# A gated mix of two attention blocks: the last output tile in pieces of 512, 256, 128 and 128 columns

## Chip, cores and metric

The kernel runs on one core of a Trainium2 chip. The metric is the device time of one execution in microseconds (us); less is better. The median of four runs before the change is 482.8 us (482.68 to 483.35).

## What is computed

The input is 2048 rows of 1024 numbers in bf16. Two blocks read it: A, a linear attention with 32 heads of 32, and B, an attention over a window of eight keys, every second one back. Each ends in a product with its own matrix `wo`, and a gate per row mixes them.

```python
def reference(A_x, A_wqkv, A_wo, B_x, B_wqkv, B_wo, gate_w):
    ...
    x = A_x
    g = _sigmoid((x * gate_w).sum(-1, keepdims=True))
    a = _A_ref(x, A_wqkv, A_wo)
    b = _B_ref(x, B_wqkv, B_wo)
    return g * a + (1 - g) * b
```

Both `_A_ref` and `_B_ref` end in `o.reshape(B, S, D) @ wo`. The change touches the last step alone: block B's product with its `wo`, and the sum of both blocks.

## The kernel before, in words

**Stages.** The rows are held transposed, features on the 128 partitions. The kernel computes B's values, queries and keys, then A's keys and values in stretches shared with B's window attention, then A's numerators. `a_out` (line 1722) makes A's gated output and leaves it in `pq0` and `xT`. `final(t)` (line 1736) makes 128 rows of the result and stores them. There are NT = 16 such tiles; the first five are built before the last calls of `a_out`, and tiles 5 to 15 (line 1801) close the program.

**One tile.** `final` cuts the tile's 1024 columns into parts. For each part TensorE (PE) runs eight matmuls that sum over the eight chunks of 128 features into one PSUM bank (line 1747; `qT` holds B's attention output, `ws[3]` holds B's `wo`). Each matmul has a weight load of 128 x 128 of its own, so a part is 16 instructions for PE, however many columns it has. VectorE (DVE) then computes bank times (1 - gate) plus A's part into an SBUF tile `o` (lines 1751 to 1754). A DMA (line 1757) writes `o` to the output. Tiles 0 to 14 have two parts of 512 columns and one DMA of 1024 columns, issued by SyncE (SP). The last tile has three parts, 512, 256 and 256, and a DMA for each: SP issues the first two, ScalarE (ACT) the third, because line 1757 gives ACT the part that ends at column 1024. Each first column has a semaphore of its own (`chan="out%d_%d"`).

**Order.** `Prog.schedule` (line 122) lays all operations out on a model clock, by the costs written beside them, and each engine gets its list in that order. `plan` runs six times, and the layout with the shortest modelled span is kept (lines 1811 to 1816). PSUM banks come from `Pool.next`; from line 1644 on there are eight of them.

**The tail.** A flag says whether a fast way of computing is allowed for this input; if it isn't, a general path of many instructions runs. Each engine's program therefore ends in a branch (lines 1820 to 1834):

```python
    def tail(e, eng, rest):
        reg = e.alloc_register("fast_ok")
        e.wait_ge(*flag_op.val)
        e.reg_load(reg, flag[0:1, 0:1])
        with e.If_eq(reg, 0):
            rest()
            ...
            for th in progs[eng]:
                th(e)
        with e.Else():
            rest()
            if eng == "sp":
                for s, v in P.last:
                    e.wait_ge(s, v)
```

`rest()` is what of the engine's list starts in the last microseconds of the modelled span, so many as `BACK` (line 22) has: 19 for SP, 14 for DVE, 30 for ACT. Operations before that are issued ahead of the branch (line 254). PE has no entry there, so all of PE's work is issued before its branch, and its `rest()` is empty. The taken side, `Else`, lies behind the general path in the program. At the end SP waits for the output DMAs (line 1834), and all engines meet at the end of the block (line 1836).

Of the kernel before, what the change touches and what calls it, by code (L numbers as in the profile page):

```python
# [1116 lines left out]
def build_kernel(nc, A_x, A_wqkv, A_wo, B_x, B_wqkv, B_wo, gate_w, out):  # L1117
    del B_x
    S = A_x.shape[1]
    NT = S // 128  # L1120
# [118 lines left out]
    def plan(seen):  # L1239
# [476 lines left out]
        def a_loc(t):  # L1716
            tgt, c0 = pqn(t // 4)
            return tgt, c0 + (t % 4) * 128
# [17 lines left out]
        def final(t):  # L1736
            tgt, c0 = a_loc(t)
            o_, os_ = osb.next()
            e_, r = t // 8, t % 8
            parts = [(0, 512), (512, 1024)] if t < NT - 1 else [(0, 512), (512, 768), (768, 1024)]  # L1740
            for f0, f1 in parts:
                bank = main.next()
                n = f1 - f0

                def fn(e, t=t, bank=bank, f0=f0, f1=f1):
                    for dc in range(8):
                        last = e.matmul(bank.ap(0, f1 - f0), qT[:, dc, t * 128:(t + 1) * 128], ws[3][:, dc, f0:f1], start=(dc == 0), stop=(dc == 7))  # L1747
                    return last
                P.op("pe", fn, 8 * mm(n), reads=[qT.part((0, 8), (t * 128, (t + 1) * 128)), ws[3].part((0, 8), (f0, f1))], writes=[bank.iv])
                i0, i1 = f0 // 128, f1 // 128  # L1750
                P.op("dve", lambda e, bank=bank, o_=o_, t=t, n=n, i0=i0, i1=i1, tgt=tgt, c0=c0: e.scalar_tensor_tensor(  # L1751
                    out=o_[:, i0 * 128:i1 * 128].rearrange("p (i s) -> p i s", s=128), in0=bank.ap(0, n).rearrange("p (i s) -> p i s", s=128),
                    scalar=gm[:, t:t + 1], in1=tgt[:, i0:i1, c0:c0 + 128], op0=ALU.mult, op1=ALU.add), dps(n),
                    reads=[bank.iv, gm.all(), tgt.part((i0, i1), (c0, c0 + 128))], writes=[o_.part((f0, f1))])
                if t == NT - 1 or f1 == 1024:
                    c = f0 if t == NT - 1 else 0
                    P.op("act" if f1 == 1024 and c else "sp", lambda e, e_=e_, r=r, o_=o_, c=c, f1=f1: e.dma_start(out2[e_, r * 128:(r + 1) * 128, c:f1], o_[:, c:f1]), 0.5,
                         reads=[o_.part((c, f1))], chan="out%d_%d" % (os_, c), lat=1.0)
# [17 lines left out]
        for t in range(EARLY):  # L1776
            while len(outs) > 16:
                a_out(*outs.pop(0))
            final(t)
# [21 lines left out]
        for t in range(EARLY, NT):  # L1801
            final(t)
# [69 lines left out]
```

## Time and profile before

| What | Value |
|---|---|
| Median of four runs | 482.8 us (482.68 to 483.35) |
| The profiled execution's own time | 483.67 us |
| Its span, first to last instruction | 481.9 us |
| Mean granted TensorE clock | 0.999 |
| PE busy | 477.6 us, 99% of the span, 4403 matmuls |
| DVE, ACT, POOL busy | 281.1, 146.5, 6.2 us |
| Matmuls of `final` (line 1747) | 264, 55.6 us |
| Additions of `final` (line 1751) | 33, of which 2 with 256 columns |
| Output DMAs (line 1757) | 17 on SP, 1 on ACT |

A row of the profile names the engine, the source line, the operation, the tile written and the tile read (`o<-ps_all` reads PSUM and writes `o`), the shape and the count. "PEld" is the weight load of TensorE, which runs beside the matmuls. A `q` behind an engine's name (`SPq`, `PEldq`) marks what the engine's sequencer does by itself: issuing DMAs, waiting for semaphores, loading a register, branching. Such instructions are not counted as busy. Times in the text are microseconds from the start of the span. The trace also holds each packet that a DMA engine moved, with its start, length and bytes; packets of kind "instruction" are pieces of the engines' own programs, fetched while they run.

### The profile page before, as it was taken

The page shows a single profiled execution, that of the slowest core. Times are in us where ns is not written, and L with a number is a line of the kernel's source. Part 1 is how long each engine was busy: PE and PEld are TensorE (multiplying, and loading weights), DVE is VectorE, ACT ScalarE, POOL GpSimd, SP SyncE. Part 2 cuts the span into 40 slices and gives each one's busy share as a digit, 9 for nine tenths or more (in the row PEclk, how much of TensorE's full clock was granted, in tenths as well). Part 3 has the DMA queues.
Part 4 walks back from the last instruction along what each step waited for, and adds up shares of the span by engine and source line. Part 5 has one row for each costly group of instructions (what it writes and reads, how often), then busy time and mean ns, then how long its engine had stood idle before and what let it go on. Part 6 is the DMA issues. An engine that isn't in the chain of part 4 may idle for free.

```text
span 481.9 us, 10218 instructions
## 1 busy us (share of the span) xinstructions
PE 477.6 (99%) x4403; PEld 224.5 (47%) x4403; DVE 281.1 (58%) x578; ACT 146.5 (30%) x234; POOL 6.2 (1%) x38
## 2 busy tenths in 40 slices
PE   8999999999999999999999999999999999999997
PEld 3444444444444544545454455444444444444443
DVE  3121436888587788566747465588588136653444
ACT  1111111135333345434434435255532130111000
POOL 4000000000000000000000000000000000000000
PEclk9999999999999999999999999999999999999999
DMA  9999994132014337432313447820194019830212
GB/s 208 252 210 311 293 353 131 44 112 87 1 31 143 87 91 147 95 81 54 88 38 92 99 123 163 236 45 2 18 246 132 0 19 242 220 23 3 88 68 90
DMA packets 72951, 57.39 MB, mean 119 GB/s; under 512 B 37953, under 2 KB 60865, under 8 KB 72898
## 3 DMA queue, kind: packets, MB, share of 16 engines
q1 hardware_dynamic: 72210, 56.07, 45.2%
q8 instruction: 36, 0.59, 0.5%
q10 hardware_dynamic: 688, 0.59, 0.4%
q14 instruction: 17, 0.14, 0.1%
HBM read 34.49 MB, written 13.76 MB: 100 GB/s over the span
## 4 chain that ended last, share of the span: by engine, by line
PE 99%; DVE 0%; issue 0%
PE ps_all L1344 81%; PE ps_all L1747 11%; PE ps_all L1464 2%; PE ps_all L1499 2%; PE ps_all L1383 1%; PE ps_all L1588 1%; PE ps_all L1692 0%; PE ps_all L1664 0%; DVE o L1751 0%; DVE warm L1290 0%
## 5 line engine op out<-in xcount | busy, mean ns | idle before, releaser
L1344 PE MATMUL ps_all<-w,xT 128*128 128x512 bf16 x960 | 211.5, 380 | 0.0
L1344 PE MATMUL ps_all<-xT,w 128*128 128x512 bf16 x768 | 168.3, 379 | 0.0
L1344 PEld LDWEIGHTS ps_all<-w,xT 128*128 128x128 bf16 x960 | 92.7, 98 | 110.9 <-issue 1.4
L1344 PEld LDWEIGHTS ps_all<-xT,w 128*128 128x128 bf16 x768 | 74.1, 98 | 89.4 <-issue 1.3
L1747 PE MATMUL ps_all<-w,qT 128*128 128x512 bf16 (+1 forms) x264 | 55.6, 373 | 0.0
L1747 PEld LDWEIGHTS ps_all<-w,qT 128*128 128x128 bf16 x264 | 25.8, 98 | 29.7
L1355 DVE TENSOR_SCALAR e<-e 128x512 bf16<-128x512 bf16 x64 | 18.5, 289 | 32.2 <-ACT e L1353 17.4
L1478 ACT ACTIVATE E<-ps_all 128x1824 bf16<-128x1824 f32 (+1 forms) x18 | 30.4, 1687 | 19.0 <-PE ps_all L1499 19.0
L1375 DVE CAST vst<-ps_all 128x512 bf16<-128x512 f32 x16 | 11.1, 694 | 42.4 <-PE ps_all L1344 42.4
L1751 DVE SCALAR_TENSOR_TENSOR o<-ps_all,gm,xT 128x512 bf16<-128x512 f32 (+1 forms) x25 | 18.0, 728 | 21.1 <-PE ps_all L1747 21.0
L1353 ACT ACTIVATE e<-ps_all 128x512 bf16<-128x512 f32 x32 | 19.1, 597 | 31.4 <-PE ps_all L1344 31.4
L1351 ACT ACTIVATE e<-ps_all 128x512 bf16<-128x512 f32 x32 | 19.1, 597 | 26.0 <-PE ps_all L1344 24.8
L1302 DVE TENSOR_TENSOR mx<-mx,kT 128x1024 bf16<-128x1024 bf16 x32 | 20.9, 685 | 9.2 <-ACT kT L1376 9.0
L1516 DVE TENSOR_TENSOR ot<-ps_all,rs 128x480 bf16<-128x480 f32 (+1 forms) x54 | 25.8, 505 | 0.0
L1302 DVE TENSOR_TENSOR mx<-mx,qT 128x1024 bf16<-128x1024 bf16 x32 | 21.0, 684 | 7.3 <-ACT qT L1379 7.1
L1376 ACT ACTIVATE az<-ps_all 128x512 bf16<-128x512 f32 x23 | 13.8, 599 | 36.3 <-PE ps_all L1344 36.3
L1376 ACT ACTIVATE vst<-ps_all 128x512 bf16<-128x512 f32 x16 | 9.6, 599 | 48.1 <-PE ps_all L1344 48.1
L1376 ACT ACTIVATE kT<-ps_all 128x512 bf16<-128x512 f32 x21 | 12.5, 597 | 36.8 <-PE ps_all L1344 36.8
L1379 ACT ACTIVATE qT<-ps_all 128x512 bf16<-128x512 f32 x19 | 11.3, 597 | 35.3 <-PE ps_all L1344 35.3
L1515 DVE RECIPROCAL rs<-ps_all 128x15 f32<-128x15 f32 (+1 forms) x54 | 9.4, 202 | 21.3 <-PE ps_all L1499 19.4
L1357 DVE SCALAR_TENSOR_TENSOR pk<-ps_all,e 128x512 bf16<-128x512 f32 x32 | 21.6, 677 | 0.1
L1379 ACT ACTIVATE xT<-ps_all,g 128x512 bf16<-128x512 f32 x10 | 6.9, 687 | 45.1 <-PE ps_all L1344 42.4
(73 smaller groups left out, 276.5 us busy)
## 6 DMA issues: line engine op xcount, KB each, us to landing
rb<-rc_hbm SPq DMA_DIRECT2D x32, 256.0 KB, 5.9
w<-in_A_wqkv_dram SPq DMA_DIRECT2D x6, 1024.0 KB, 9.4
v<-vB_hbm SPq DMA_DIRECT2D x36, 132.0 KB, 2.7
vB_hbm<-vst SPq DMA_DIRECT2D x32, 132.0 KB, 5.5
w<-in_B_wqkv_dram SPq DMA_DIRECT2D x4, 1024.0 KB, 9.8
xn<-in_A_x_dram SPq DMA_DIRECT2D x16, 256.0 KB, 2.6
out_dram<-o SPq DMA_DIRECT2D x15, 256.0 KB
oB_hbm<-ot SPq DMA_DIRECT2D x36, 96.0 KB, 2.1
```

Source lines behind the costliest of these rows:

```text
L1302: P.op("dve", lambda e, m=m, op=op: e.tensor_tensor(m[:, 0:n], m[:, 0:n], src, op), 0.08 + n / 1920.0, reads=[m.all(), reg], writes=[m.all()],
L1344: last = e.matmul(bank.ap(), lhs(dc), rhs(dc), start=(dc == 0), stop=(dc == 7))
L1351: P.op("act", lambda e: e.activation(e_[:, :], bank.ap(), ACT.Exp), act(512), reads=[bank.iv], writes=[e_.all()])
L1353: P.op("act", lambda e: e.activation(e_[:, :], bank.ap(), ACT.Exp, accum_out=qe[:, col:col + 1]), act(512) + 0.1, reads=[bank.iv], writes= ...
L1355: P.op("dve", lambda e: e.tensor_scalar(e_[:, :], e_[:, :], 1.0, 1e-6, op0=ALU.min, op1=ALU.add), 0.25, reads=[e_.all()], writes=[e_.all()])
L1357: P.op("dve", lambda e: e.scalar_tensor_tensor(out=dst, in0=bank.ap(), scalar=0.0, in1=e_[:, :], op0=ALU.max, op1=ALU.add), dps(512), read ...
L1376: fa = lambda e: e.activation(dst, src(), ACT.Copy)
L1379: fa = lambda e: e.activation(dst, src(), ACT.Copy, scale=scale)
L1478: P.op("act", lambda e: e.activation(E[:, 0:32 * nq].rearrange("p (j q) -> p j q", j=4), ps[:, 4:8, 0:8 * nq], ACT.Exp), act(32 * nq), rea ...
L1516: P.op("dve", lambda e, r=r, src=src, dst=dst, m=m: e.tensor_tensor(dst, src()[:, :, 0:32], r[:, 0:m, None].to_broadcast([128, m, 32]), AL ...
L1747: last = e.matmul(bank.ap(0, f1 - f0), qT[:, dc, t * 128:(t + 1) * 128], ws[3][:, dc, f0:f1], start=(dc == 0), stop=(dc == 7))
L1751: P.op("dve", lambda e, bank=bank, o_=o_, t=t, n=n, i0=i0, i1=i1, tgt=tgt, c0=c0: e.scalar_tensor_tensor(out=o_[:, i0 * 128:i1 * 128].rear ...
```

## The change

The last tile's second block of 512 columns is cut into 256, 128 and 128 columns in place of 256 and 256.

```diff
-            parts = [(0, 512), (512, 1024)] if t < NT - 1 else [(0, 512), (512, 768), (768, 1024)]
+            parts = [(0, 512), (512, 1024)] if t < NT - 1 else [(0, 512), (512, 768), (768, 896), (896, 1024)]
```

What follows from that one line: the part of columns 768 to 1023 becomes two groups of eight matmuls with 128 columns each in place of one group with 256; two additions of 128 columns in place of one of 256; and two DMAs of 128 rows by 256 bytes in place of one of 128 rows by 512 bytes. SP issues the one for columns 768 to 895, ACT the one for 896 to 1023. There is one more bank taken, and one more semaphore for SP to wait for at the end.

## The prediction

> **What bounds the kernel now.** The page comes first: busy time of the engines, then the chain that ended last.
>
> ```profile
> PE 477.6 (99%) x4403; PEld 224.5 (47%) x4403; DVE 281.1 (58%) x578; ACT 146.5 (30%) x234; POOL 6.2 (1%) x38
> ...
> PE 99%; DVE 0%; issue 0%
> ```
>
> TensorE fills the span, and the change leaves its columns as they are. So everything is decided behind the last matmul. The chain in order of time, from 460 us on, and the timeline of the last five microseconds show that stretch:
>
> ```profile
> 459.87 19.03 PE ps_all L1747 x96
> 478.90 0.03 issue
> 478.92 0.48 DVE o L1751
> ```
>
> ```profile
> 478.56 1.27 SPq L1757 DMA_DIRECT2D out_dram<-o  x1
> 478.92 0.48 DVE L1751 SCALAR_TENSOR_TENSOR o<-ps_all,gm,xT 128x256 bf16<-128x256 f32 x1 [0.39 <-PE ps_all L1747]
> 479.44 0.36 ACTq L1757 DMA_DIRECT2D out_dram<-o  x1
> ```
>
> The chain stops at 479.40, yet the span goes on to 481.94. The rest lies in rows that don't count as busy. Asked by source line: the branch (1824), the meeting at the end of the block (1836) and SP's wait for the stores (1834).
>
> ```profile
> L1824 DVEq COMPARE_BRANCH  x1: 72/72/72, 465.7 to 465.7; - x1
> L1824 PEldq COMPARE_BRANCH  x1: 3764/3764/3764, 477.1 to 477.1; - x1
> ```
>
> ```profile
> L1836 PEldq DRAIN  x1: 73/73/73, 480.9 to 480.9; - x1
> L1836 SPq DRAIN  x1: 13/13/13, 481.7 to 481.7; - x1
> ```
>
> ```profile
> L1834 SPq EVENT_SEMAPHORE  x2: 17/22/28, 481.4 to 481.5; - x2
> ```
>
> Two things run side by side to the end. The stores: the last one landed at 481.38, SP passed its waits at 481.40 to 481.49 and reached the meeting at 481.70. And PE's sequencer: its branch began at 477.12 and took 3.76 us, so PE reached the meeting at 480.94 and left its drain at 481.02. The stores came last, PE 0.70 us ahead of them. From the later of the two to the end of the span it was 0.22 us (481.72 to 481.94).
>
> Why 3.76 us? The trace's packets hold one of kind "instruction", 16,384 bytes, on PE's own queue at 478.49 to 479.46: 1.37 us behind the branch's start, and 1.42 us before its end. The branch jumps over the general path to code that isn't there and waits for it. The other engines show the same, hidden behind their 45 to 72 ns: DVE branches at 465.68, its fetch moves at 466.72, its next addition starts at 468.61. That 16 KB packet also hit the stores. One DMA engine carried it, and the eight 1024-byte packets that this engine had of the 512-column store ran from 479.45 to 480.16, where the others were done by 479.25. SP's next store found its queue full and was held:
>
> ```profile
> L1757 SPq DMA_DIRECT2D out_dram<-o x2: 332/800/1267, 478.0 to 478.6; - x2
> L1757 ACTq DMA_DIRECT2D out_dram<-o x1: 365/365/365, 479.4 to 479.4; - x1
> ```
>
> 332 ns is the usual price, 1267 ns that of the held one.
>
> **The change, part by part** (sums against the profiled execution: span 481.94, own time 483.67; that is 0.9 above the median of 482.8, to which I carry over the differences alone).
>
> *Matmuls.* With 512 columns one starts 216 ns after the one before, with 256 columns 109 ns, as these windows show (nine and seventeen starts):
>
> ```profile
> 475.25:476.97 1.72, 1.72 (x9) 0.78 (x8) 0.75 (x1) 0.00 (x0) 0.00 (x0) 1.00 0.00 0
> 476.97:478.72 1.75, 1.75 (x17) 1.46 (x15) 1.24 (x2) 0.00 (x0) 0.00 (x0) 1.00 0.43 159
> ```
>
> That is 0.417 ns per column and about 2.5 ns fixed, so 128 columns should start every 56 ns: 16 x 56 = 0.89 us for 8 x 109 = 0.87 us, +0.02. No row has a full weight load under 128 columns. If loads, 98 ns each, could not overlap at all, it would be 16 x 98 = 1.57 us, +0.70; below, nothing can be had, since the columns stay. I take +0.02, by the 256-column row, whose 109 ns show no trace of its 98 ns load.
>
> The Trainium skill speaks against this: "TensorE: Matmul & The Clock Gate", section "Back-to-back issue gap", gives some 81 ns for a weight load and a matmul of 128 columns. By it the estimate would be 16 x 81 = 1.30 us, +0.42.
>
> *Additions.* 749 ns with 512 columns, 484 with 256: 1.04 ns per column, so 351 ns with 128. The first of the two lies beside the last eight matmuls. The second starts 0.04 behind the last matmul as now and ends 0.13 earlier. With the matmuls: -0.11.
>
> *Stores.* ACT's store is issued 0.11 earlier. Its 128 rows shrink from 512 to 256 bytes; a 512-byte packet took 27 ns and each DMA engine has eight, so between 0 and 0.11 is saved. SP now has three stores to issue. If nothing holds them, the new one goes out at about 478.9, ahead of ACT's at 479.3, and costs nothing; if the queue is full as before, it comes behind the held one, 0.33 + 0.04 later. So the end of the stores moves by -0.5 (no store held: ACT's 479.3 plus its 1.8 us to landing is 481.1, less what the others add) to +0.4. One more semaphore for SP is satisfied or nearly so: the two it passed there took 17 and 28 ns.
>
> *PE's sequencer.* Here I see the largest term. The load of the flag stands behind all matmuls in PE's program. It ran at 476.56, when 17 matmuls had still to start; PE's waits in earlier tiles (454.12, 457.57, ... 471.38) also run 17 matmuls ahead of the group they guard. So the sequencer runs ahead by a fixed number of instructions, not by a time. Before, those 17 are one of 512 and sixteen of 256 columns, 2.16 us of work up to the last end less its drain. After, they are one of 256 and sixteen of 128: the flag's load follows the start of the seventh matmul of the 256-column group, 476.97 + 6 x 0.109 = 477.63, so 477.65 in place of 476.56. The branch comes **1.09 us later**, at 478.21, and with its 3.76 us ends at 481.97; drain 482.10; plus 0.22 gives a span of 482.32, **+0.39**. The 0.70 us that PE was ahead is used up, and PE is last. The cover is thus gone by 0.39, whatever the stores gain. If the branch is bound to something else (the end of PE's queue, say), this term is 0.
>
> *A fetch more.* PE's 16 KB packets came at 372.62, 398.08, 429.45 and 451.97. I count the instructions dispatched 1.1 us before each (the usual distance from a branch to its packet): loads, matmuls and PE's own, started, plus the 33 that stand ready. It gives 7,857, 8,118, 8,411 and 8,626: about 256 apart, with one that came late. The next border is at 8,877 to 8,882. The branch stands at 8,871 before, so the border was never reached; the change adds 16 instructions (eight loads, eight matmuls), and the branch stands at 8,887. So a fetch in sequence probably starts shortly before the branch (by 0.3 to 0.9 us), useless, and the branch's own fetch comes behind it. Its packet would move at 478.4 to 479.4, the branch's at 479.6 to 480.55. Even side by side, two such packets on one DMA engine can hold the stores by up to a microsecond: 0 to +0.95 on the end, with the +0.39 inside it.
>
> The skill's page "Runtime: NRT & Kernel Launch", section "Instruction fetch mechanics", says that a taken branch out of the fetched window stalls for the target's block, which the 3.76 us agree with, and calls the crossing of a block border mostly hidden; by it the extra fetch would cost nothing, and the sum would stay at +0.39.
>
> **Forecast.** PE's branch ends last, 1.09 later: +0.39, and up to +0.95 with stores held by the second packet. Median 482.8 + 0.5 = 483.3. A measurement of this kernel can tell about 0.2% (0.97 us) from no change, so this counts as no change. Chance 0.48; nearly all of it within the bound.
>
> **Rivals.**
>
> *The fetches queue up, and the kernel is slower (0.36).* Place: PE's instruction fetch between 477.4 and the end. If PE can't ask for the branch's block until the useless block is complete, the branch waits for both. The first is asked for at 477.3 to 477.5, and by the branch's own 3.76 us is in place at about 480.8 (0.97 of packet, 1.4 on either side). A second round of 1.04 + 0.97 + 1.42 = 3.4 us ends at 484.2, drain and meeting at 484.5: +2.6 on the span, 485.4 by the median, 485.1 to 485.8 with the spread of such packets (0.88 to 1.46 us). For it: behind each branch the next block's fetch came only after the engine had gone on (PE: 480.88, then 481.62), so I see no two at once. Against it: no row shows a branch meeting a fetch in flight. It decides from the point where the border lies ahead of the branch: ten instructions fewer and it is gone.
>
> *The stores decide, and the kernel gains a little (0.13).* PE's branch isn't delayed, or its fetch misses the stores. Then the end moves by -0.1 to -0.5: 482.3 to 482.7. For it: the stores are last today. Against it: the fixed lead of 17 matmuls.
>
> *More than that (0.03).* All of what lies between the addition and the landing is 2 us and mostly fixed, so a gain over 0.97 has no place here; I leave 0.03 for an effect that I don't see. That the change reorders the plan is excluded by its costs: the modelled span shrinks by 0.11, and no operation starts within 0.11 of the borders where SP, DVE and ACT branch; earlier banks are taken in the same order.
>
> **How the numbers follow.** Forecast 483.3 (0.48), slower rival (0.36), small gain (0.13), larger gain (0.03). Range 482.6 to 485.7: from the small gain's nearer half to the slower rival, of which the topmost tenth is left out. Without the slower rival the forecast's own range is 483.1 to 483.8. Faster by over 0.2%: 0.03. Within: 0.48 + 0.13 less 0.04 for the forecast's upper edge: 0.57. Slower: 0.36 + 0.04 = 0.40.
>
> **What would show it.** PE's flag load at 477.65 and its branch at 478.2; its duration, 3.8 (forecast) or over 6 us (rival); one or two 16 KB packets on PE's queue between 478 and 481; PE's drain behind SP's or ahead of it at the meeting; the last matmul's start at 478.69 if 56 ns hold, later if loads bind; the additions at 351 ns; and whether SP's second and third store are held. I am wrong if PE's branch starts where it did, or if the time falls by more than 0.5 us.

## The result and the profile after

The changed kernel takes 483.53 us (median of 40 runs, 482.79 to 484.30), the kernel before 482.91 (60 runs): a ratio of 1.0013, 95% interval 1.0009 to 1.0018. That is +0.62 us, slower by less than the 0.2% named in the prediction, but clear of the noise.

The two profiled spans hide it: 481.9 us before, 481.8 after. The profiled execution before was a late one (483.67 against a median of 482.91), the one after an average one (483.56). What comes before the last tile drifts from run to run (the last tile's first store left at 477.95 and 477.07 in two profiles of the kernel before), so I compare **tails**: from the moment SP issues the last tile's 512-column store (477.95 before, 477.66 after) to the end of the span. That store is the same instruction in all kernels here. The tail was 3.98 us before (3.80 in the second profile, number 5) and is 4.13 us after. That is 0.15 to 0.33 us of the 0.62; the profiles don't show where the rest lies.

TensorE and the additions first. Windows of the changed kernel, from the first 256-column matmul and from the first 128-column one (columns: time, then busy time and count of PE, weight loads, DVE):

```profile
476.68:477.55 0.87, 0.87 (x9) 0.78 (x8) 0.67 (x1) 0.00 (x0) 0.00 (x0) 1.00 0.79 301
477.55:478.44 0.89, 0.89 (x18) 0.88 (x15) 0.77 (x3) 0.00 (x0) 0.00 (x0) 1.00 0.00 0
```

Sixteen matmuls of 128 columns take 0.89 us, 56 ns each, with a 98 ns weight load beside each. The chain of the changed kernel ends in an addition of 0.35 us:

```profile
478.62 0.03 issue
478.65 0.35 DVE o L1751
```

So the pieces do what they should. Now the rows that don't count as busy: PE's flag load and branch, the meeting at the end of the block, SP's waits for the stores, and the stores' issue, each asked by its source line.

```profile
L1823 PEldq TENSOR_LOAD <-flag x1: 492/492/492, 477.4 to 477.4; - x1
```

```profile
L1824 PEldq COMPARE_BRANCH  x1: 3364/3364/3364, 477.9 to 477.9; - x1
```

```profile
L1836 PEldq DRAIN  x1: 72/72/72, 481.3 to 481.3; - x1
L1836 SPq DRAIN  x1: 13/13/13, 481.6 to 481.6; - x1
```

```profile
L1834 SPq EVENT_SEMAPHORE  x2: 28/28/28, 481.1 to 481.3; - x2
```

```profile
L1757 SPq DMA_DIRECT2D out_dram<-o x3: 332/332/430, 477.7 to 478.6; - x3
L1757 ACTq DMA_DIRECT2D out_dram<-o x1: 370/370/370, 479.0 to 479.0; - x1
```

PE's flag load came 0.30 us ahead of the tail's start, and 1.39 ahead of it before: 1.09 us later, as predicted. No store is held at its issue any more (332 to 430 ns; 1267 before). Yet they land late. The trace's packets say why. PE's 16 KB of code moved at 478.94 to 479.91, 1.03 us behind the branch. Before, the same packet moved 0.54 us behind the tail's start and met the first of the three stores; now it moves 1.28 us behind it and meets the three that follow. Of the 128 row packets of each of these three stores, 120 were done by 480.17. The other eight of each came one behind the other after the code packet, as on one DMA engine of sixteen, from 479.90 to 480.64, and the last landing came at 481.29. The packets between 478.5 and 480.7 show these last ones as single digits on the right of the GB/s row; q8 is PE's code, and the last figure of an `out_dram` row is the time from issue to landing:

```profile
DMA  6999997900058975100268510279630000000000
GB/s 223 317 317 447 317 335 243 429 19 0 19 177 251 289 196 158 28 0 0 65 158 187 117 33 0 61 158 196 145 56 9 9 0 9 9 9 19 19 9 0
...
q8 instruction: 1, 0.02, 2.8%
...
out_dram<-o SPq DMA_DIRECT2D x1, 64.0 KB, 2.7
out_dram<-o SPq DMA_DIRECT2D x1, 32.0 KB, 2.5
out_dram<-o ACTq DMA_DIRECT2D x1, 32.0 KB, 2.3
```

PE left its drain at 481.40, SP at 481.57: SP was still last, by 0.16 us.

### The profile page after: what moved, and what is told of

The parts are those of the page before. It is cut to its first block, busy times and chain, and to the rows that moved or that the text cites. A ratio compares the mean times of both kernels' runs of the same rounds, so it can differ in the third digit from the quotient of the medians.

```text
span 481.8 us, 10236 instructions
## 1 busy us (share of the span) xinstructions
PE 477.3 (99%) x4411; PEld 224.6 (47%) x4411; DVE 281.7 (58%) x579; ACT 146.7 (30%) x234; POOL 6.2 (1%) x38
## 4 chain that ended last, share of the span: by engine, by line
PE 99%; DVE 0%; issue 0%
PE ps_all L1344 81%; PE ps_all L1747 11%; PE ps_all L1464 2%; PE ps_all L1499 2%; PE ps_all L1383 1%; PE ps_all L1588 1%; PE ps_all L1692 0%; PE ps_all L1664 0%; DVE o L1751 0%; DVE warm L1290 0%
## 5 line engine op out<-in xcount | busy, mean ns | idle before, releaser
L1747 PE MATMUL ps_all<-w,qT 128*128 128x512 bf16 (+2 forms) x272 | 55.6, 366 | 0.0
L1751 DVE SCALAR_TENSOR_TENSOR o<-ps_all,gm,xT 128x512 bf16<-128x512 f32 (+2 forms) x26 | 18.2, 708 | 20.8 <-PE ps_all L1747 20.5
```

## The experiments

Two theories. **Theory**: PE's branch, 1.09 us later because 16 more instructions stand ahead of it, is the loss, either through PE's own late arrival or through the code packet that it calls for. **Rival**: the smaller and more numerous stores are the loss. Times are medians of 11 runs (5 in number 6), ratios are against the kernel before on the same chip; those medians were 482.92 to 483.08.

**1. Spare matmuls: the branch later, the stores as before.**

```diff
         for t in range(EARLY, NT):
             final(t)
+        spare = main.next()
+        def spare_fn(e):
+            for dc in range(8):
+                last = e.matmul(spare.ap(0, 128), qT[:, dc, (NT - 1) * 128:NT * 128], ws[3][:, dc, 0:128], start=(dc == 0), stop=(dc == 7))
+            return last
+        P.op("pe", spare_fn, 8 * mm(128), reads=[...], writes=[spare.iv])
```

> The kernel before, with eight spare matmuls of 128 columns behind the last ones; they write a bank that nobody reads, and no store or addition changes. They add 16 instructions to PE's program, as the change does, so PE's flag load should again follow the seventh matmul of the first 256-column group, 1.09 us later than before. Theory (PE's later branch and its code fetch are the loss): 483.3 to 483.6, as with the change. Rival (the smaller and more numerous stores are the loss): 482.9, as before.

Measured: 483.52, ratio 1.0014 (1.0005 to 1.0023). The whole loss appears with the old stores and additions. The branch came 0.24 us behind the tail's start, against 0.25 with the change and 0.83 ahead of it before. The one profile, of the fastest of the 11 runs, has a tail of 3.99 us, hardly over the two of the kernel before, and PE left its drain 0.02 us behind SP; so the loss is shown here by the time, not by the profile.

**2. The last store in two, matmuls and additions as before.**

```diff
-                    P.op("act" if f1 == 1024 and c else "sp", ...
+                    for c, f1 in [(c, f1)] if c < 768 else [(768, 896), (896, 1024)]:
+                        P.op("act" if f1 == 1024 and c else "sp", ...
```

> The kernel before with its matmuls and additions; only the store of the last 256 columns is cut into two of 128, the first issued by SP, the second by ACT, as in the changed kernel. PE's program is that of before, its branch at the old place. Theory (PE's branch): 482.8 to 483.1. Rival (stores): 483.5, or more, since both wait for the 256-column addition.

Measured: 483.33, ratio 1.0008 (0.9999 to 1.0017). This lies between the two and its interval reaches both. The issue rows of this kernel name a price of its own: the packet at its old place holds the 256-column store (1258 ns), and SP's third store must go out behind it.

```profile
L1758 SPq DMA_DIRECT2D out_dram<-o x3: 332/450/1258, 477.4 to 479.3; - x3
```

With the change SP's third store went out at 478.64, 0.98 behind the tail's start; here at 1.91. So this is no pure count of stores, and the times don't settle what these two stores cost.

**3. The fine matmuls, but one store for the last 256 columns.**

```diff
-                if t == NT - 1 or f1 == 1024:
-                    c = f0 if t == NT - 1 else 0
+                if t == NT - 1 and f1 != 896 or f1 == 1024:
+                    c = min(f0, 768) if t == NT - 1 else 0
```

> The changed kernel with its matmuls and additions in pieces of 128, but one store for the last 256 columns, issued by ACT behind the last addition, as before. PE's branch stays 1.09 us late. Theory (PE's branch): 483.3 to 483.6, as with the change. Rival (stores): 482.8, a little under the kernel before, since the last addition ends 0.1 us earlier.

Measured: 483.44, ratio 1.0011 (1.0001 to 1.0020). With three stores as before and PE's program long, the loss stays, so smaller and more stores aren't needed for it. The rival is out as the main cause. In its profile PE's branch took 3.80 us, and the tail was 4.41 us:

```profile
L1836 PEldq DRAIN  x1: 73/73/73, 481.4 to 481.4; - x1
L1836 SPq DRAIN  x1: 13/13/13, 481.4 to 481.4; - x1
```

Here PE and SP arrived together (PE 0.02 us later), so this profile can't say which of them sets the end. Number 12 takes PE's wait away.

**4. PE's branch ahead of the last six groups.**

```diff
-BACK = {"sp": 19, "dve": 14, "act": 30}
+BACK = {"sp": 19, "dve": 14, "act": 30, "pe": 9.5}
```

> The changed kernel with PE's branch moved ahead: the last six groups (three of 512 columns, then 256, 128, 128) are issued behind it, as the other engines do with their own last operations. The fetch then moves some 7 us before the end. Theory (PE's branch): the loss goes, and the gain of the smaller pieces shows: 482.3 to 482.8; less if PE runs dry, since 17 matmuls of 216 ns are 3.7 us of cover for 0.55 of flag load and 3.4 to 3.8 of branch (up to 0.6 us, then 482.8 to 483.2). Rival (stores): 483.5 still.

Measured: 483.15, ratio 1.0008 (0.9998 to 1.0017). The tail fell to 3.36 us, but PE ran dry behind its branch. The additions of its profile stand 1.73 us apart, and once 2.18:

```profile
471.20 0.75 DVE L1751 SCALAR_TENSOR_TENSOR o<-ps_all,gm,xT 128x512 bf16<-128x512 f32 x1 [0.98 <-PE ps_all L1747]
473.38 0.75 DVE L1751 SCALAR_TENSOR_TENSOR o<-ps_all,gm,xT 128x512 bf16<-128x512 f32 x1 [1.44 <-PE ps_all L1747]
```

That is a hole of 0.46 us: 0.55 of flag load and 3.62 of branch are longer than what is queued.

**5. Control: the kernel before, unchanged.**

> The kernel before, unchanged, as a control: what a measurement tells where nothing differs, and a second profile of the tail. 482.9, ratio 1.0000 within 0.0010. If it comes out 0.1% slower itself, the losses measured so far are not the change's.

Measured: 482.84, ratio 1.0002 (0.9993 to 1.0011). Its profile gives a second tail of the kernel before, 3.80 us.

**6. Sixteen spare matmuls.** The edit of number 1 with sixteen of them.

> The kernel before with sixteen spare matmuls of 128 columns behind the last ones in place of eight. PE's flag load should come when 17 matmuls have still to start: at the last real one, some 1.95 us later than before, 0.9 later than with eight. Theory (the loss is PE's later branch): the branch's end now sets the end alone, 483.6 to 484.3, more than with eight spares. Rival (any change of the program costs the same 0.1%): 483.4 to 483.5 again.

Measured: 484.77, ratio 1.0037 (1.0023 to 1.0050), +1.84 us, more than the theory said. That any change of the program costs the same 0.1%, the rival here, is out. The packets between 478 and the end of this kernel's span show two pieces of code in place of one, and landings 1.4 us later after their issue than before (2.8 and 1.8):

```profile
q8 instruction: 2, 0.03, 3.0%
...
out_dram<-o SPq DMA_DIRECT2D x1, 64.0 KB, 4.2
out_dram<-o ACTq DMA_DIRECT2D x1, 64.0 KB, 3.2
```

The first moved at 478.12 to 479.32, and so began before the branch could ask for one (478.95); I take it for the next block in sequence. The second moved at 480.00, 1.04 us behind the branch. And the branch:

```profile
L1831 PEldq COMPARE_BRANCH  x1: 3702/3702/3702, 479.0 to 479.0; - x1
```

3.70 us, the usual length, with the other fetch in flight when it began. So in this profile the second fetch didn't make the branch longer, and the stores landed late. At the meeting:

```profile
L1843 PEldq DRAIN  x1: 73/73/73, 482.7 to 482.7; - x1
L1843 SPq DRAIN  x1: 13/13/13, 482.8 to 482.8; - x1
```

PE left its drain at 482.79 and SP at 482.84. Only 0.05 us lie between them, so this run doesn't say which of the two the loss goes through.

**7 and 8. Early branch with the flag loaded two groups earlier, fine and coarse pieces.** 7 is the changed kernel, 8 the kernel before.

```diff
+BACK = {..., "pe": 9.5}
...
-            go(e, ops[:k])
-            tail(e, eng, lambda: go(e, ops[k:]))
+            j = k - (2 if eng == "pe" else 0)
+            go(e, ops[:j])
+            tail(e, eng, lambda: go(e, ops[j:k]), lambda: go(e, ops[k:]))
...
         e.reg_load(reg, flag[0:1, 0:1])
+        ahead()
```

> The changed kernel with PE's branch ahead of the last six groups, and the flag's load two groups ahead of the branch, so that PE's dispatch stands still for the branch's 3.4 to 3.8 us alone, beside 3.7 us of queued matmuls. Theory (PE's branch): no or little idle time on PE, and the tail of the early branch (0.6 us less from the last tile's first store to the end than before): 482.2 to 482.6. Rival (stores): 483.5.

> The kernel before (512, 256, 256) with the same early load and early branch of PE. Against the finer pieces with the early branch this shows what the pieces are worth when PE's branch is out of the way. Theory: 482.4 to 482.8, and 0.1 to 0.3 above the finer pieces, since the last addition ends later by 0.11 and its store is larger. Rival (stores): 482.9, and faster than the finer pieces.

Measured: 7 took 482.99, ratio 1.0001 (0.9992 to 1.0010); 8 took 483.18, ratio 1.0004 (0.9995 to 1.0013). The fine pieces lose their loss; neither kernel beats the one before. Tails 3.37 and 3.62: the pieces are worth 0.25 there. In 7 the branch took 3.93 us and left a hole of 0.23; in 8 it took 3.61 and left none. The rival missed 7 by 0.5 us, and its order of the two kernels came out the other way in the medians; the theory missed the size of both by 0.4.

**9 and 10. No far jump: PE's side of the general path is empty.** 9 is the changed kernel, 10 the kernel before; both leave out what PE would compute if the flag were 0.

```diff
-            for s, v in P.final + [(P.esem[x], n) for x, n in P.counts.items() if n]:
+            for s, v in P.final + [(P.esem[x], n) for x, n in P.counts.items() if n] if eng != "pe" else []:
                 e.wait_ge(s, v)
-            for th in progs[eng]:
+            for th in progs[eng] if eng != "pe" else []:
```

> The changed kernel without PE's share of the general path: the side of the branch that isn't taken is empty on PE, so the branch's target lies a few instructions on, in code that PE should hold already. This leaves out what PE would compute if the flag were 0, which it isn't here; all that runs is the same. Theory (PE's later branch and its fetch): no fetch for the branch, PE far ahead at the meeting, no store held; 482.3 to 482.6, below the kernel before. If the code's own order still calls for a block at the end, the packet hits the stores: 482.7 to 483.2. Rival (stores): 483.5, as with the change.

> The kernel before (512, 256, 256) without PE's share of the general path, in the same way. Theory: its branch costs it something too, since the packet held a store of SP (1267 for 332 ns); without it 482.5 to 482.8, and 0.1 to 0.3 above the finer pieces without it. Rival (stores): 482.9, as before.

Measured: 9 (fine) took 482.85, ratio 0.9995 (0.9986 to 1.0004); 10 (coarse) took 483.15, ratio 1.0000 (0.9991 to 1.0009). The theory had promised more: 482.3 to 482.6 for 9 and 482.5 to 482.8 for 10, missed by 0.25 and 0.35. The rival missed 9 by 0.65. With the far jump gone, the same matmuls, additions and stores as in the changed kernel cost nothing against the kernel before. The branch of 9, and its landings:

```profile
L1824 PEldq COMPARE_BRANCH  x1: 229/229/229, 478.2 to 478.2; - x1
```

```profile
out_dram<-o SPq DMA_DIRECT2D x1, 64.0 KB, 1.6
out_dram<-o SPq DMA_DIRECT2D x1, 32.0 KB, 1.6
out_dram<-o ACTq DMA_DIRECT2D x1, 32.0 KB, 1.5
```

No piece of code moved near the end, and the last three stores landed 1.5 to 1.6 us after their issue; with the change the same three took 2.7, 2.5 and 2.3. The tails are 3.36 and 3.61: again 0.25 for the pieces.

**11. Early branch, some 21 us ahead.** The edit of number 7 with `"pe": 23`.

> The changed kernel with PE's branch and the flag's load still earlier, some 21 us ahead of the end of the modelled plan, general path and all. If the branch ahead of the last groups gained nothing because PE ran dry for 0.2 to 0.5 us behind it, the same is to be seen here: 482.8 to 483.2, with a hole in the matmuls behind the branch as long as the branch is over 3.7 us. If it was instead a packet of a later block that came at the end, the time falls here to 482.3 to 482.6.

Measured: 482.94, ratio 0.9998 (0.9989 to 1.0007), with a tail of 3.36 and a hole of 0.05 us. The general path is whole here, so this is the changed kernel in a usable form without its loss: its interval and the change's (1.0009 to 1.0018) don't meet. It doesn't measurably beat the kernel before.

**12. The packet without PE's wait.** As number 9, but the hundred or so waits on PE's side stay.

```diff
-            for th in progs[eng]:
+            for th in progs[eng] if eng != "pe" else []:
```

> The changed kernel without PE's products of the general path, as before, but with PE's list of some hundred waits of that side kept (it leaves out what PE would compute if the flag were 0, which it isn't here). The branch's target lies a hundred instructions on, probably in the next block, which PE should hold; entering it should call for the block after it. So the 16 KB packet comes at the stores, while PE doesn't wait for it. If the packet alone holds the end up: 1.0 us behind the branch a packet, the stores landing 0.5 to 0.8 later than with an empty side, PE's drain early, 483.2 to 483.5. If PE's late arrival is what counts: 482.7 to 483.0, as with the empty side.

Measured: 484.06, ratio 1.0017 (1.0008 to 1.0026), a loss, and 0.56 us over the range that was given for it. The branch was short and PE was early, but one piece of code moved 1.03 us behind the branch and 1.27 behind the tail's start (1.28 with the change), and the stores landed late. Branch, meeting and landings of this kernel:

```profile
L1824 PEldq COMPARE_BRANCH  x1: 358/358/358, 477.4 to 477.4; - x1
```

```profile
L1836 PEldq DRAIN  x1: 341/341/341, 477.8 to 477.8; - x1
...
L1836 SPq DRAIN  x1: 13/13/13, 481.2 to 481.2; - x1
```

```profile
q8 instruction: 1, 0.02, 1.5%
...
out_dram<-o SPq DMA_DIRECT2D x1, 64.0 KB, 2.7
out_dram<-o SPq DMA_DIRECT2D x1, 32.0 KB, 2.5
out_dram<-o ACTq DMA_DIRECT2D x1, 32.0 KB, 2.4
```

The tail is 4.22 us. PE was ready 3 us ahead of SP, and the loss is whole. Against number 9, which has the same work and no packet, the last three stores landed 0.9 to 1.1 us later after their issue. So the packet alone is enough to hold up the end; PE's own arrival isn't needed for it. This doesn't show that PE's arrival adds nothing in the changed kernel.

## Why the prediction was right, point by point

**The number.** 483.3 was forecast as no change within 0.2%, with 483.1 to 483.8 as that case's own range; 483.53 was measured. The sign of the small loss and its size (+0.5 forecast, +0.62 measured) held. That the size fits is in part luck: the +0.5 is +0.39 of PE's arrival with a share for a second packet, and the second packet never came, while PE's arrival wasn't what ended last in the profile.

**Matmuls and additions: right.** 56 ns per matmul of 128 columns and 351 ns per addition, both worked out from the larger shapes. The 81 ns that the Trainium skill gives ("TensorE: Matmul & The Clock Gate", section "Back-to-back issue gap") does not hold for this stream; the measured 56 ns decides. ACT's store went out 0.11 us earlier, as forecast (1.37 us behind the tail's start in place of 1.48).

**The lead of 17 matmuls: right.** The branch came 1.09 us later with the change. Eight spare matmuls in the old kernel moved it just as far and brought the whole loss (number 1).

**PE's branch ends last: the step that failed in its reason.** The prediction put the loss at PE's own arrival at the meeting, with a branch of 3.76 us and 0.22 us ahead of the end of the span, and had the stores held as an extra of up to 0.95. In the profile of the change the branch took 3.36 us. PE's end moved by 0.68 us against the tail's start (from 3.06 to 3.75), not by 1.09, SP's by 0.15 (from 3.76 to 3.91), and SP was still last by 0.16. With the code packet but without PE's wait the loss was as large (number 12); with neither it was gone (number 9). The held stores, priced "0 to +0.95 with the +0.39 inside it", are thus enough for the whole of it. PE's arrival stands close behind them, since the same fetch delays both. In numbers 1 and 3 it was 0.02 us behind SP's, and branches took up to 3.93 us here, so PE may end last in other executions of the changed kernel; what its arrival adds there stays open.

**The stores: the range was loosely worked out.** ACT's 479.3 plus 1.8 us is 481.1, which is 0.3 ahead of the old last landing and not 0.5. With no packet near them the last landing did come 0.56 us earlier against the tail's start (2.87 in number 9, 3.43 before); with the change it came 0.21 later (3.64). That SP's queue was full is a reading: the rows show an issue of 1267 ns with the packet and of 333 without it (number 10).

**A fetch more: wrong here, and the count was short.** One piece of code moved near the end, not two. The border that I set at 6 to 11 instructions behind the old branch lies further: 16 more instructions didn't reach it, 32 did (number 6). A packet that PE doesn't wait for isn't free either: in number 12 one came, and the time rose by 0.98 us.

**The slower rival: refuted, as far as one profile goes.** Where two fetches did come (number 6), the branch took its usual 3.70 us; the rival needed over 6. The kernel with two packets lost 1.84 us, with the stores and PE arriving 0.05 us apart.

**The small gain: seen in the tails, not in the times.** Finer pieces shorten the tail by 0.25 us when no code moves there (3.36 against 3.61, and 3.37 against 3.62, one profile each). Of it 0.11 is ACT's earlier issue and 0.14 the quicker landing of its smaller store (1.50 us in place of 1.64), where the prediction had 0 to 0.11. 9 against 10 differs by 0.30 in the median, but their intervals overlap. The change gives this and pays more for the packet's new place.

**Open.** The kernel before has a packet in its tail too, and its two profiled tails (3.98, 3.80) are longer than the coarse kernel's without one (3.61, 3.62). Yet taking it away gained nothing measurable (numbers 8 and 10; their intervals reach down to 0.9995 and 0.9991, 0.2 and 0.4 us, so a gain of the size of the tails isn't excluded). The finer pieces without a packet have tails 0.4 to 0.6 us shorter than the kernel before and still no lower time clear of the noise (numbers 7, 9 and 11), and the change's own loss is larger than its tail shows. A tail comes from one execution each, and what precedes it drifts; whether the usual tail of the kernel before is shorter than those two is not settled.

## What to carry to other kernels

When the last step is cut finer, ask what every engine's program does there besides the work: the sequencer's lead counts in instructions, so small instructions behind the last large ones move a branch, and the code that it calls for, closer to the end. Look at the instruction packets in the trace beside the last stores: here one packet of 16 KB delayed eight of the 128 row packets of each store behind it, and the last landing came 0.65 us after the last of these. A jump over code that is never run belongs where stores aren't on the path, and with enough queued work to cover it (number 11; in number 4 the cover was 0.46 us short).

## What the runs showed of the hardware that was not expected

- PE's branch to code that isn't there took 3.36 to 3.93 us in eleven profiles, with its packet 1.0 to 1.6 us behind its start; to code a few instructions on 0.23 us, to code some hundred on 0.36.
- A branch took its usual 3.70 us though another piece of code was still moving when it began (number 6, one profile).
- A piece of code also moved where PE didn't wait for it and the program was about to end (number 12: 1.03 us behind a branch of 0.36 us), and it cost more than the finer pieces gained. I read it as the block behind the one that PE had just entered; the trace doesn't name what a packet holds.
- Code also moves behind the end. In number 8 a packet came 1.83 us after the span's end. The time outside the span was 2.6 us in this execution and 3.2 in another, and 1.7 to 1.9 in the other nine, where the other kernels have 1.7 to 1.8. Its ratio is therefore no clean measure of its tail.
